# Cross-attention and a leaky-ReLU layer on one core: the state placed by matmuls, its load put behind x, and the copies of the first microseconds dealt out anew

## The chip, the core and the metric

The kernel runs on one core of a Trainium2 chip. The core has a matrix engine (TensorE; its rows in the profile are PE, and PEld for the loading of its weights), a vector engine (VectorE, DVE), a scalar engine (ScalarE, ACT), a general engine (GpSimd, POOL) and an engine that only issues transfers (SyncE, SP). Each works through its own list of instructions in order; semaphores order them against each other. TensorE writes to a small memory, PSUM, of eight banks for each of 128 partitions; VectorE and ScalarE copy its results on into the large memory, SBUF. Transfers (DMAs) between the chip's main memory and SBUF are issued by SP, ACT or POOL and carried out by 16 DMA engines. The metric is the time of one run in microseconds (us) on the device. A smaller time is better.

## The reference, cut to what matters

```python
B, H, S, Ns, D = (8, 8, 512, 32, 64)         # x: B,H,S,D   state: B,H,Ns,D
scores  = scale * x @ state^T                # softmax over the 32 state rows
xread   = softmax(scores)  @ state           # B,H,512,64
scores2 = scale * state @ x^T                # softmax over the 512 positions
sread   = softmax(scores2) @ x               # B,H,32,64
t = concat([xread, sread], axis=2), heads side by side   # (4352, 512)
h = t @ w_in                                 # w_in 512 x 2048
out = max(0.01 * h, h) @ w_out               # w_out 2048 x 512
```

All inputs and the output are fp32; the matmuls run on bf16 copies.

## The kernel before, in words

**Algebra.** The rows of `xread` are never formed. For each batch the kernel first makes M = state @ w_in, head by head, (`a_m`, in four column chunks of 512, each evicted by `m_evict`), and then h = softmax(scores) @ M (FF1). FF1 of one batch is 16 steps of 128 hidden columns; each result goes through a leaky ReLU on ScalarE into `hT`. The second matmul (FF2) is cut into pieces: `piece(b, hT, i, jq)` does four matmuls, a quarter jq of the sum for 128 output rows i, and with jq = 3 copies the finished 128 x 512 tile out and stores it. The `sread` rows of all batches are gathered and go through both layers at the end.

**Order.** The order is written by hand: inside `tc.manual_schedule` each engine runs its instructions as the program lists them. Batch 0 has its own opening (lines 403 to 554) and batch 1 its own passage (lines 556 to 597), because there is nothing yet to hide their softmax behind. Then comes FF1 of batch 1, in a loop of 16 steps that prepares batch 2 (lines 604 to 633), and from batch 2 on a regular loop. This change touches what runs up to the end of that first loop, near 63 us. The rest is the same in both kernels.

**Buffers.** A tile pool hands out buffers by tag. Tiles of one tag take turns in the pool's `bufs` buffers, and a tile that gives no tag goes by its name. The pool `consts` has `bufs=1`. So the two halves of batch 0's x, `xf[0]` and `xf[1]` (heads 0 to 3 and 4 to 7, 512 KB each, lines 62 to 68), have a buffer each, by the tags `xf0` and `xf1`. The whole state in fp32, `stf`, has the tag `xf1` too (line 110), and its load, which SP issues, comes after the casts that read `xf[1]`. PSUM is dealt out in the same way: tags `py` and `ph` with two banks of one tile each, `big` and `sc` with one tile of two banks each.

**Opening of batch 0.** ACT loads the state of batch 0 (`st0f`); SP loads `xf[0]` and `xf[1]`; POOL then issues the weights by a queue of its own, in this order: `w_in` chunks 0 and 1, 2 and 3, `w_out` chunk 0, x of batch 1, `w_out` 1, and later `w_out` 2 and 3 and x of batch 2. `spin` issues matmuls on zeros. `state0` transposes batch 0's state and places it in two forms: `st0_t`, heads stacked, and `stbd`, two heads as a block diagonal with zeros between (cleared by a memset). For each half u of x: `cast_x0` makes bf16, `x0_half` transposes it on TensorE, `xt0_evict` copies the transpose to SBUF, `scores0` multiplies it with `stbd`, and `max0`, `sub0`, `exp0`, `probs0` do the softmax. `at0_t` transposes the probabilities for FF1; the second half's feed the matmuls with g = 1 (`ff1_0(ph, 0, (1,))`, line 534). `a_scores(a0)` and `a_max2(a0)` begin the softmax over positions.

**State of all batches.** POOL casts `stf` twice into `stb` (line 538); within FF1 of batch 0 `state_t` transposes it in 16 matmuls, and VectorE copies it into `st_t` in two halves (line 154). Batch 1's M needs `st_t`.

**Batch 1.** M chunk 0, the cast of x, 16 transposes of x into one `big` tile, two copies to `xT`, the scores, the softmax (`a_shift`, `a_exp`, `a_probs`) and M chunks 1 to 3 stand between the FF2 pieces of batch 0. `a_probs(a1)` must be done before FF1 of batch 1.

Of the kernel before, what the change touches and what calls it, by code (L numbers as in the profile page):

```python
# [9 lines left out]
P = 128  # L10
B, H, S, D = 8, 8, 512, 64
NS = 32
# [3 lines left out]
NT = S // P  # L16
NK = H // 2
# [10 lines left out]
def kernel(  # L28
# [30 lines left out]
    nc.scalar.dma_start(  # L59
        st0f[:], state[0].rearrange("h n d -> (h n) d").rearrange("(p r) d -> p r d", r=2)  # L60
    )
    xf = [
        consts.tile([P, NK, 2 * P], FP32, name="xf", tag="xf0"),
        consts.tile([P, NK, 2 * P], FP32, name="xf", tag="xf1"),
    ]
    xv = x[0].rearrange("h (p t) d -> p h (t d)", t=NT)
    for u in range(2):
        nc.sync.dma_start(xf[u][:], xv[:, NK * u:NK * (u + 1)])

    idle = consts.tile([P, S], BF16, name="idle")  # L70
    nc.vector.memset(idle[:], 0.0)  # L71
    stbd = consts.tile([P, NK, 2, NS], BF16, name="stbd")
    nc.vector.memset(stbd[:], 0.0)
    warm = consts.tile([P, 2], FP32, name="warm")
    nc.vector.memset(warm[:], 0.0)
    nc.scalar.activation(out=warm[:], in_=warm[:], func=AF.Exp)
    ident = consts.tile([P, P], BF16, name="ident")
    make_identity(nc, ident[:])

    w_in_bf = wpool.tile([P, NK, DFF], BF16, name="w_in_bf")  # L80
    w_out_bf = wpool.tile([P, 16, DM], BF16, name="w_out_bf")
# [25 lines left out]
            moe_w_in[:, DM * c:DM * (c + 1)].rearrange("(k p) f -> p k f", p=P),  # L107
        )

    stf = consts.tile([P, 16, D], FP32, name="stf", tag="xf1")  # L110

    def load_state():
        nc.sync.dma_start(
            stf[:], state.rearrange("b h n d -> (b h n) d").rearrange("(p r) d -> p r d", r=16)
        )

    def load_w_out(c):
        nc.gpsimd.dma_start(
            w_out_bf[:, 4 * c:4 * (c + 1), :],
# [7 lines left out]

    st0_t = consts.tile([P, P], BF16, name="st0_t")  # L130
    st_t = consts.tile([P, B, P], BF16, name="st_t")
    sr_t = consts.tile([P, NK, B * NS], BF16, name="sr_t")

    def state0():
        stb0 = consts.tile([P, 2, 2, D], BF16, name="stb0")
        nc.gpsimd.tensor_copy(stb0[:], st0f[:, :, None, :].to_broadcast([P, 2, 2, D]))
        ps = psum.tile([P, 2, P], BF16, name="pst0", tag="big", bufs=1)
        for r in range(2):
            nc.tensor.transpose(ps[:, r, :], stb0[:, r].rearrange("p g d -> p (g d)"), ident[:])
        for g in range(2):  # L140
            rows = slice(D * g, D * (g + 1))
            src = ps[rows].rearrange("p r (k g q) -> p k g q r", k=NK, g=2)[:, :, g]
            VEC(stbd[rows, :, g].rearrange("p k (q r) -> p k q r", r=2), src)
            SCA(st0_t[rows, :].rearrange("p (k q r) -> p k q r", k=NK, r=2), src)

    stb = consts.tile([P, 16, 2, D], BF16, name="stb")

    def state_t():
        ps = psum.tile([P, 16, P], BF16, name="pst", tag="big", bufs=1)
        for r in range(16):  # L150
            nc.tensor.transpose(ps[:, r, :], stb[:, r].rearrange("p g d -> p (g d)"), ident[:])
        for g in range(2):
            rows = slice(D * g, D * (g + 1))
            nc.vector.tensor_copy(
                st_t[rows].rearrange("p b (k q r) -> p (b k) q r", k=NK, q=2),
                ps[rows].rearrange("p r (c g q) -> p c g q r", g=2, q=2)[:, :, g],
            )

# [25 lines left out]
        a_xt_pe(a, a.pxt, 0, NT)  # L186

    def st_of(a, g, k):
        rows, cols = slice(D * g, D * (g + 1)), slice(NS * k, NS * (k + 1))
        return st0_t[rows, cols] if a.b == 0 else st_t[rows, a.b, cols]  # L190

    def a_scores(a):
        sc = psum.tile([P, 2, S], FP32, name="sc", tag="sc", bufs=1)
# [208 lines left out]

    open_xb(0)
    a_open(a0, 0)
    spin(5, "py")
    state0()
    spin(4, "py")

    def x0_half(u):
        pxt = [psum.tile([P, NT, P], BF16, name="pxth", tag="ph") for _ in range(2)]  # L410
        for v in range(2):
            for t in range(NT):
                h = NK * u + 2 * v
                nc.tensor.transpose(
                    pxt[v][:, t, :], a0.xb[:, t, h:h + 2, :].rearrange("p h d -> p (h d)"), ident[:]
                )
        return pxt

    def xt0_evict(u, pxt):
        for v, copy in ((0, VEC), (1, SCA)):  # L420
            copy(a0.xT[:, :, 2 * u + v, :], pxt[v][:])

    sct = psum.tile([P, 2, NG, NS], FP32, name="sct", tag="sc", bufs=1)

    def scores0(u):
        for t in range(NT):
            for v in range(2):
                c = NK * t + 2 * v
                nc.tensor.matmul(
                    sct[:, u, c:c + 2, :].rearrange("p c n -> p (c n)"),  # L430
                    lhsT=a0.xT[:, t, 2 * u + v, :],
                    rhs=stbd[:, 2 * u + v].rearrange("p g n -> p (g n)"),
                    start=True, stop=True,
                )
# [36 lines left out]
    load_w_in(0)  # L471
    load_w_in(1)
    cast_x0(0, 2, VEC)
    cast_x0(2, 3, SCA)
    cast_x0(3, 4, POO)
    pxt = x0_half(0)
    xt0_evict(0, pxt)
    cast_x0(4, 6, VEC)
    cast_x0(6, 7, SCA)
    cast_x0(7, 8, POO)  # L480
    for c in range(2, 4):
        load_w_in(c)
    load_state()
    load_w_out(0)
    load_x(1, nc.gpsimd)
    load_w_out(1)
    scores0(0)
    pxt = x0_half(1)
    m = max0(0)
    xt0_evict(1, pxt)  # L490
    sub0(0, m)
    scores0(1)
    exp0(0)
    sub0(1, max0(1))
    spin(2, "ph")

    m_evict(a0, 0, a_m(a0, 0, "py"), SCA)
    exp0(1)
    spin(6, "ph")
    a_scores(a0)  # L500
    probs0(0)
    a0.aT = att.tile([P, 2, S], BF16, name="aT", tag="aT")
    pat = psum.tile([P, 2, 2 * S], BF16, name="pat", tag="big", bufs=1)
    at0_t(0, 0, NT, pat[:, 0])
    SCA(a0.aT[:, 0], pat[:, 0, :S])
    probs0(1)
    pm = a_m(a0, 1, "py")
    spin(2, "ph")

# [14 lines left out]

    ph = [psum.tile([P, S], FP32, name="ph", tag="ph")[:] for _ in range(2)]
    ff1_0(ph, 0, (0,))
    at0_t(1, 0, 2, pat[:, 0, S:])
    at0_t(1, 2, NT, pat[:, 1])  # L530
    VEC(a0.aT[:, 1, :2 * P], pat[:, 0, S:S + 2 * P])
    SCA(a0.aT[:, 1, 2 * P:], pat[:, 1, :2 * P])
    m_evict(a0, 1, pm, VEC)
    ff1_0(ph, 0, (1,))
    act_0(ph, 0)
    a_max2(a0)
    for g in range(2):
        POO(stb[:, :, g], stf[:])
    for c in range(2, 4):
        load_w_out(c)  # L540
    for j in range(2, 16, 2):
        if j % 4 == 2 and j < 12:
            pr = psum.tile([P, 2, S], FP32, name="php", tag="big", bufs=1)
            ff1_0([pr[:, 0], pr[:, 1]], j)
            nc.scalar.activation(out=h0[:, j:j + 2, :], in_=pr[:], func=AF.Prelu, alpha=0.01)
        else:
            ph = [psum.tile([P, S], FP32, name="ph", tag="ph")[:] for _ in range(2)]
            ff1_0(ph, j)
            act_0(ph, j)
        if j in (2, 6):  # L550
            c = 2 + j // 4
            m_evict(a0, c, a_m(a0, c, "py"), VEC)
        if j == 12:
            state_t()

    tags = ("py", "py", "ph", "ph")
    open_xb(1)
    a_open(a1, 1)
    for i in (0, 1):
        piece(0, h0, i, 0, tags[i])  # L560
    m_evict(a1, 0, a_m(a1, 0, "big"), SCA)
    for g in range(2):
        a_exp2(a0, g)
    cast_x(1, 0, 3, POO)
    cast_x(1, 3, 6, VEC)
    cast_x(1, 6, 8, SCA)
    load_x(2, nc.gpsimd)
    for i in (2, 3):
        piece(0, h0, i, 0, tags[i])
    a_xt_full(a1)  # L570
    VEC(a1.xT[:, 0:2], a1.pxt[:, 0:2])
    SCA(a1.xT[:, 2:4], a1.pxt[:, 2:4])
    piece(0, h0, 0, 1, tags[0])
    a_scores(a1)
    m_evict(a1, 1, a_m(a1, 1, "big"), SCA)
    a_shift(a1)
    a_max2(a1)
    for i in (1, 2):
        piece(0, h0, i, 1, tags[i])
    m_evict(a1, 2, a_m(a1, 2, "big"), SCA)  # L580
    a_exp(a1)
    a_probs(a1)
    for i, jq in ((3, 1), (0, 2)):
        piece(0, h0, i, jq, tags[i])
    m_evict(a1, 3, a_m(a1, 3, "big"), SCA)
    for g in range(2):
        a_exp2(a1, g)
    a_probs2(a0)
    a_a2t(a0)
    for i, jq in ((1, 2), (2, 2), (3, 2), (2, 3), (3, 3)):  # L590
        piece(0, h0, i, jq, tags[i], VEC if i % 2 else SCA)
    a_probs2(a1)
    a_a2t(a1)
    open_xb(2)
    cast_x(2, 0, 5, POO)
    cast_x(2, 5, 8, VEC)
    a_open(a2, 2)


# [5 lines left out]
    for s in range(16):  # L605
# [4 lines left out]
        if s == 2:  # L610
            a_xt_full(a2)
            VEC(a2.xT[:], a2.pxt[:])
        elif s == 4:
            a_scores(a2)
            m_evict(a2, 0, a_m(a2, 0, "big"), SCA)
            a_shift(a2)
            a_max2(a2)
            cast_x(3, 0, 8, POO)
        elif s == 7:
            m_evict(a2, 1, a_m(a2, 1, "big"), SCA)  # L620
        elif s == 8:
            a_exp(a2)
        elif s == 9:
            a_sread(a0)
        elif s in (10, 11):
            a_exp2(a2, s - 10)
            if s == 11:
                a_probs(a2)
                a_probs2(a2)
        elif s == 12:  # L630
            m_evict(a2, 2, a_m(a2, 2, "big"), SCA)
            a_open(att_of[3], 3)
            a_xt_dma(att_of[3])

# [99 lines left out]
```

## Time and profile before

| | us |
|---|---|
| median of three runs | 227.44 |
| the runs | 226.44, 227.44, 227.64 |
| the profiled execution | 227.53 |
| its span, first to last instruction | 225.8 |
| TensorE busy | 211.6 (94%) |
| ScalarE busy | 140.4 (62%) |
| VectorE busy | 102.9 (46%) |
| GpSimd busy | 23.9 (11%) |

A line of the timeline gives the start in us, the duration in us (of a group: from its first start to its last end), the engine, the line of the kernel, the operation, what is written and read, how many of them, and in brackets how long the engine stood idle before it and who released it. SPq, POOLq and ACTq are the issuing of transfers; their own duration is the issue, not the transfer. A line of waits gives the engine and line that waited, who ended the wait, the total in us, how often, and the longest.

### The profile page before, as it was taken

What the parts mean: (1) busy time and instruction counts of PE and PEld (TensorE: products, weight loads), DVE (VectorE), ACT (ScalarE), POOL (GpSimd) and SP (SyncE); (2) the same over time, 40 slices, a digit from 0 to 9 for tenths busy, and PEclk for the clock granted to TensorE, in tenths of its full rate; (3) what the DMA queues carried; (4) which work ended last, traced back from release to release, by engine and by line L of the source; (5) the groups of instructions that cost most, each with busy time, mean ns of one, the idle gap of its engine ahead of it and who ended that gap; (6) DMA issues with size and microseconds to landing.
All of it is one profiled execution on the core that took longest, in us unless ns stands there. A gap on an engine that the chain in (4) does not pass through costs nothing.

```text
span 225.8 us, 3512 instructions
## 1 busy us (share of the span) xinstructions
PE 211.6 (94%) x1411; PEld 98.4 (44%) x1437; DVE 102.9 (46%) x151; ACT 140.4 (62%) x262; POOL 23.9 (11%) x28
## 2 busy tenths in 40 slices
PE   7689978899899999999999999999999999999994
PEld 2333433344344444444444444444443444456653
DVE  2688428977846732673268327832782100000000
ACT  3448765658976846684668566865686465554420
POOL 5842202000221003000300030000000000000000
PEclk9889999999999999999999999999999999999999
DMA  6999990098591198119811892191213021102113
GB/s 195 186 250 273 221 281 6 1 194 274 103 270 46 49 202 216 49 46 184 235 49 46 168 218 83 46 163 26 93 51 93 0 93 49 46 1 92 49 46 93
DMA packets 35311, 27.02 MB, mean 120 GB/s; under 512 B 19808, under 2 KB 30432, under 8 KB 35296
## 3 DMA queue, kind: packets, MB, share of 16 engines
q1 hardware_dynamic: 30384, 20.45, 34.6%
q0 software_dynamic: 4768, 6.29, 13.9%
q8 instruction: 11, 0.18, 0.3%
q10 hardware_dynamic: 144, 0.07, 0.1%
q14 instruction: 4, 0.03, 0.1%
HBM read 17.37 MB, written 8.91 MB: 116 GB/s over the span
## 4 chain that ended last, share of the span: by engine, by line
PE 82%; ACT 7%; DVE 6%; DMA 2%; issue 2%; SPq 1%; POOL 0%; ACTq 0%; DVEq 0%
PE py L365 45%; PE ph L337 20%; PE pm L316 4%; PE ph L348 3%; PE pspin L126 2%; PE ph L518 2%; PE psr L290 1%; ACT M L330 1%; ACT hT L342 1%; PE sc L196 1%; DMA st0f<-in_state_dram 1%; ACT e L264 1%; PE pxt L178 1%; PE php L518 1%; DMA out_dram<-ysb 1%
## 5 line engine op out<-in xcount | busy, mean ns | idle before, releaser
L365 PE MATMUL py<-w_out_bf,hT 128*128 128x512 bf16 x478 | 122.9, 379 | 2.0 <-issue 1.3
L342 ACT ACTIVATE hT<-ph 128x512 bf16<-128x512 f32 x112 | 67.2, 602 | 45.4 <-PE ph L337 45.4
L365 PEld LDWEIGHTS <-hT 128*128 128x128 bf16 x496 | 46.3, 98 | 57.3 <-issue 6.6
L337 PE MATMUL ph<-aT,M 128*128 128x512 bf16 x218 | 65.0, 379 | 2.1 <-ACT hT L342 1.0
L337 PEld LDWEIGHTS <-M 128*128 128x128 bf16 x224 | 21.5, 98 | 28.8 <-issue 3.6
L371 ACT COPY ysb<-py 128x512 f32<-128x512 f32 x31 | 18.2, 586 | 11.6 <-PE py L365 11.6
L92 POOL CAST xb<-xl 128x2048 bf16<-128x2048 f32 (+2 forms) x7 | 11.6, 1653 | 104.7 <-DMA xl<-in_x_dram 75.2
L330 DVE CAST M<-pm 128x1024 bf16<-128x1024 f32 x10 | 12.3, 1225 | 21.9 <-PE pm L316 21.9
L393 DVE COPY ysh<-pyh 128x256 f32<-128x256 f32 x1 | 0.4, 424 | 44.8 <-PE pyh L388 44.8
L330 ACT CAST M<-pm 128x1024 bf16<-128x1024 f32 x18 | 18.2, 1013 | 3.8 <-PE pm L316 3.8
L206 DVE TRANSPOSE_TENSOR_REDUCE mrow<-sc 128x32 f32<-128x1024 f32 x7 | 8.8, 1250 | 23.2 <-PE sc L196 23.1
L228 DVE TRANSPOSE_TENSOR_REDUCE r<-e 128x32 f32<-128x1024 bf16 x7 | 8.7, 1244 | 10.7 <-ACT e L223 10.7
L316 PE MATMUL pm<-w_in_bf,st_t 64*32 64x512 bf16 x256 | 13.3, 389 | 0.0
L264 ACT ACTIVATE e<-sc,mcols 128x512 bf16<-128x512 f32 x16 | 11.1, 698 | 0.0
L256 DVE TENSOR_REDUCE mcol<-sc 128x2 f32<-128x1024 f32 x8 | 9.7, 1214 | 0.0
L126 PE MATMUL pspin<-idle 128*128 128x512 bf16 x18 | 7.7, 569 | 1.5 <-DVE idle L71 1.2
L352 ACT ACTIVATE hs<-ph 128x256 bf16<-128x256 f32 x16 | 6.0, 385 | 4.6 <-PE ph L348 4.4
L237 DVE STREAM_TRANSPOSE qb<-qh 128x1024 bf16<-128x1024 bf16 x7 | 8.7, 1246 | 0.2
L214 DVE STREAM_TRANSPOSE mrowb<-mrow 128x1024 f32<-128x1024 f32 x7 | 8.7, 1245 | 0.2
L216 DVE TENSOR_TENSOR sh<-sc,mrowb 128x1024 f32<-128x1024 f32 x7 | 8.6, 1224 | 0.2
L348 PE MATMUL ph<-sr_t,w_in_bf 128*128 128x256 bf16 x64 | 8.3, 273 | 0.0
L223 ACT ACTIVATE e<-sh 128x1024 bf16<-128x1024 f32 x7 | 7.4, 1051 | 0.4 <-DVE sh L216 0.4
(80 smaller groups left out, 144.3 us busy)
## 6 DMA issues: line engine op xcount, KB each, us to landing
out_dram<-ysb SPq DMA_DIRECT2D x31, 256.0 KB, 2.3
xl<-in_x_dram SPq DMA_DIRECT2D x5, 1024.0 KB, 7.0
w_in_bf<-in_moe_w_in_dram POOLq DMA_DIRECT2D x4, 512.0 KB, 8.2
w_out_bf<-in_moe_w_out_dram POOLq DMA_DIRECT2D x4, 512.0 KB, 14.1
xl<-in_x_dram POOLq DMA_DIRECT2D x2, 1024.0 KB, 12.6
xf<-in_x_dram SPq DMA_DIRECT2D x2, 512.0 KB, 4.6
stf<-in_state_dram SPq DMA_DIRECT2D x1, 512.0 KB, 6.4
out_dram<-ysb SPq DMA_DIRECT2D x8, 64.0 KB, 1.7
```

The costliest lines, as they stand in the source:

```text
L92: copy(xs[b][:, :, h0:h1].rearrange("p t h d -> p h t d"), xl[b][:, h0:h1].rearrange("p h (t d) -> p h t d", t=NT),)
L126: nc.tensor.matmul(p[:], lhsT=idle[:, :P], rhs=idle[:], start=True, stop=True)
L206: nc.vector.tensor_reduce(out=m1[:], in_=flat.rearrange("p (c j) -> p c j", j=NS), axis=AX.X, op=ALU.max, apply_transpose=True,)
L256: nc.vector.tensor_reduce(out=m2[:], in_=a.sc[:], axis=AX.X, op=ALU.max, negate=True)
L264: nc.scalar.activation(out=a.e2[:, g], in_=a.sc[:, g, :], func=AF.Exp, bias=a.m2s[:, g:g + 1], scale=SCALE, accum_out=a.r2[:, g:g + 1],)
L316: nc.tensor.matmul(at[v][NS * r:NS * (r + 1)], lhsT=st_of(a, g, k), rhs=w_in_bf[D * g:D * (g + 1), k, DM * c:DM * (c + 1)], start=True, st ...
L330: copy(a.M[:, :, cols], pm[:])
L337: nc.tensor.matmul(ph[:], lhsT=a.M[:, g, P * j:P * (j + 1)], rhs=a.aT[:, g, :], start=(g == 0), stop=(g == 1),)
L342: nc.scalar.activation(out=hT[:, j, :], in_=ph[:], func=AF.Prelu, alpha=0.01)
L348: nc.tensor.matmul(ph[:, :n], lhsT=w_in_bf[:, k, P * j:P * (j + 1)], rhs=sr_t[:, k, :], start=(k == 0), stop=(k == NK - 1),)
L365: nc.tensor.matmul(y.py[:], lhsT=hT[:, j, P * i:P * (i + 1)], rhs=w_out_bf[:, j, :], start=(j == 0), stop=(j == 15),)
L371: copy(ysb[:], y.py[:])
```

## The change

- `xf[0]` and `xf[1]` are given no tag; `stf` is given a tile of its own, and SP issues its load directly behind the two of x.
- `state0`: POOL casts `st0f` once; `identg` holds, for each g, the identity with the columns of the other heads set to zero (made on POOL); four matmuls against it replace two transposes, and one copy by ScalarE replaces two by VectorE and two by ScalarE. `st0_t` and the memset of `stbd` go; `st_of` reads `stbd` for batch 0.
- `state_t`: 32 matmuls with columns of the identity replace 16 transposes, into the tag `sc`; they stand ahead of batch 0's first `at0_t`. ScalarE makes `stb` in one cast in place of POOL's two, and `state_evict` is one VectorE copy within FF1 of batch 0.
- Batch 0's x: ScalarE casts heads 2 and 3; VectorE casts heads 4 to 6, POOL head 7. The halves' transposes use different PSUM tags; `scores0` runs through the first pair of heads before the second. Spins are moved.
- `a_scores(a0)` and `a_max2(a0)` move into FF1 of batch 0 (j = 8), as do chunks 0 and 1 of batch 1's M (j = 10 and 12), evicted by VectorE.
- Batch 1's x is transposed in two halves, in `big` and `sc`; `a_probs2(a0)` and the transpose by DMA behind it move to the end of the pieces, and `a_probs(a1)` ahead of six of them.
- `w_out` 1 to 3 and x of batch 2 are issued by POOL directly behind x of batch 1. POOL alone casts x of batch 2.
- In FF1 of batch 1, batch 2's M chunks 1 and 2 move from steps 7 and 12 (ScalarE) to 12 and 14 (VectorE).

```diff
-    xf = [
-        consts.tile([P, NK, 2 * P], FP32, name="xf", tag="xf0"),
-        consts.tile([P, NK, 2 * P], FP32, name="xf", tag="xf1"),
-    ]
+    xf = [consts.tile([P, NK, 2 * P], FP32, name="xf") for _ in range(2)]
     xv = x[0].rearrange("h (p t) d -> p h (t d)", t=NT)
     for u in range(2):
         nc.sync.dma_start(xf[u][:], xv[:, NK * u:NK * (u + 1)])
+    stf = consts.tile([P, 16, D], FP32, name="stf")
+    nc.sync.dma_start(
+        stf[:], state.rearrange("b h n d -> (b h n) d").rearrange("(p r) d -> p r d", r=16)
+    )
...
+    identg = consts.tile([P, 2, P], BF16, name="identg")
+    nc.gpsimd.memset(identg[:], 0.0)
+    for g in range(2):
+        nc.gpsimd.tensor_copy(
+            identg[:, g].rearrange("p (k v q) -> p k v q", k=NK, v=2)[:, :, g],
+            ident[:].rearrange("p (k v q) -> p k v q", k=NK, v=2)[:, :, g],
+        )
...
-    stf = consts.tile([P, 16, D], FP32, name="stf", tag="xf1")
...
     def state0():
-        stb0 = consts.tile([P, 2, 2, D], BF16, name="stb0")
-        nc.gpsimd.tensor_copy(stb0[:], st0f[:, :, None, :].to_broadcast([P, 2, 2, D]))
-        ps = psum.tile([P, 2, P], BF16, name="pst0", tag="big", bufs=1)
+        ps = psum.tile([P, 2, P], FP32, name="pst0", tag="big", bufs=1)
         for r in range(2):
-            nc.tensor.transpose(ps[:, r, :], stb0[:, r].rearrange("p g d -> p (g d)"), ident[:])
-        for g in range(2):
...
+            for g in range(2):
+                nc.tensor.matmul(
+                    ps[D * g:D * (g + 1), r, :], lhsT=stb0[:, r, :], rhs=identg[:, g, :],
+                    start=True, stop=True,
+                )
+        SCA(
+            stbd[:].rearrange("p k g (q r) -> p (k g) q r", r=2),
+            ps[:].rearrange("p r (h q) -> p h q r", q=16),
+        )
...
     def state_t():
-        ps = psum.tile([P, 16, P], BF16, name="pst", tag="big", bufs=1)
+        ps = psum.tile([P, 16, D], FP32, name="pst", tag="sc", bufs=1)
         for r in range(16):
-            nc.tensor.transpose(ps[:, r, :], stb[:, r].rearrange("p g d -> p (g d)"), ident[:])
...
+            for g in range(2):
+                nc.tensor.matmul(
+                    ps[D * g:D * (g + 1), r, :].rearrange("p (c q) -> p c q", q=2),
+                    lhsT=stb[:, r, :],
+                    rhs=ident[:].rearrange("p (c v q) -> p c v q", v=2, q=2)[:, :, g],
+                    start=True, stop=True,
+                )
+        return ps
+
+    def state_evict(ps, copy):
+        copy(
+            st_t[:].rearrange("p b (k q r) -> p (b k) q r", k=NK, q=2),
+            ps[:].rearrange("p r (c q) -> p c q r", q=2),
+        )
...
-    spin(5, "py")
+    POO(stb0[:], st0f[:])
+    spin(6, "py")
     state0()
-    spin(4, "py")
+    spin(3, "py")
...
     cast_x0(0, 2, VEC)
-    cast_x0(2, 3, SCA)
-    cast_x0(3, 4, POO)
+    cast_x0(2, 4, SCA)
     pxt = x0_half(0)
-    xt0_evict(0, pxt)
-    cast_x0(4, 6, VEC)
-    cast_x0(6, 7, SCA)
+    xt0_evict(0, pxt, (VEC, SCA))
+    cast_x0(4, 7, VEC)
     cast_x0(7, 8, POO)
     for c in range(2, 4):
         load_w_in(c)
-    load_state()
     load_w_out(0)
     load_x(1, nc.gpsimd)
-    load_w_out(1)
+    for c in range(1, 4):
+        load_w_out(c)
+    load_x(2, nc.gpsimd)
     scores0(0)
     pxt = x0_half(1)
     m = max0(0)
-    xt0_evict(1, pxt)
+    xt0_evict(1, pxt, (SCA, VEC))
     sub0(0, m)
+    spin(2, "ph")
     scores0(1)
     exp0(0)
+    SCA(stb[:], stf[:])
     sub0(1, max0(1))
-    spin(2, "ph")
+    exp0(1)
+    spin(5, "ph")
 
     m_evict(a0, 0, a_m(a0, 0, "py"), SCA)
-    exp0(1)
-    spin(6, "ph")
-    a_scores(a0)
+    pst = state_t()
     probs0(0)
...
-    spin(2, "ph")
...
     ff1_0(ph, 0, (0,))
-    at0_t(1, 0, 2, pat[:, 0, S:])
-    at0_t(1, 2, NT, pat[:, 1])
-    VEC(a0.aT[:, 1, :2 * P], pat[:, 0, S:S + 2 * P])
-    SCA(a0.aT[:, 1, 2 * P:], pat[:, 1, :2 * P])
+    at0_t(1, 0, NT, pat[0][:, 1])
+    VEC(a0.aT[:, 1], pat[0][:, 1, :S])
     m_evict(a0, 1, pm, VEC)
     ff1_0(ph, 0, (1,))
     act_0(ph, 0)
-    a_max2(a0)
-    for g in range(2):
-        POO(stb[:, :, g], stf[:])
-    for c in range(2, 4):
-        load_w_out(c)
+    open_xb(1)
+    a_open(a1, 1)
...
-        if j == 12:
-            state_t()
+            if j == 2:
+                state_evict(pst, VEC)
+        elif j == 8:
+            a_scores(a0)
+            a_max2(a0)
+        elif j in (10, 12):
+            c = (j - 10) // 2
+            m_evict(a1, c, a_m(a1, c, ("py", "big")[c]), VEC)
...
-    for i in (2, 3):
+    for i in (0, 1, 2):
         piece(0, h0, i, 0, tags[i])
-    a_xt_full(a1)
-    VEC(a1.xT[:, 0:2], a1.pxt[:, 0:2])
-    SCA(a1.xT[:, 2:4], a1.pxt[:, 2:4])
-    piece(0, h0, 0, 1, tags[0])
+    for t0, tag, copy in ((0, "big", VEC), (2, "sc", SCA)):
+        ps = psum.tile([P, 2, NK, P], BF16, name="pxt2", tag=tag, bufs=1)
+        a_xt_pe(a1, ps, t0, t0 + 2)
+        copy(a1.xT[:, t0:t0 + 2], ps[:])
+    piece(0, h0, 3, 0, tags[3])
     a_scores(a1)
...
     a_exp(a1)
-    a_probs(a1)
...
     for g in range(2):
         a_exp2(a1, g)
+    a_probs(a1)
+    for i, jq in ((0, 2), (1, 2), (2, 2), (3, 2), (2, 3), (3, 3)):
+        piece(0, h0, i, jq, tags[i], VEC if i % 2 else SCA)
     a_probs2(a0)
     a_a2t(a0)
...
-    cast_x(2, 0, 5, POO)
-    cast_x(2, 5, 8, VEC)
+    cast_x(2, 0, 8, POO)
...
-        elif s == 7:
-            m_evict(a2, 1, a_m(a2, 1, "big"), SCA)
...
-        elif s == 12:
-            m_evict(a2, 2, a_m(a2, 2, "big"), SCA)
-            a_open(att_of[3], 3)
-            a_xt_dma(att_of[3])
+        elif s in (12, 14):
+            c = s // 2 - 5
+            m_evict(a2, c, a_m(a2, c, "big"), VEC)
+            if s == 12:
+                a_open(att_of[3], 3)
+                a_xt_dma(att_of[3])
```

## The prediction

> **What bounds the kernel now.** I read the page's busy shares and slices first, then the timeline of the first 63 us, the landings of each load, and TensorE's waits from 17 to 64 us.
>
> ```profile
> PE   7689978899899999999999999999999999999994
> DVE  2688428977846732673268327832782100000000
> PEclk9889999999999999999999999999999999999999
> ```
>
> From about 63 us TensorE is full, and nothing the change touches runs there. All it can move is the stretch before: an opening, up to 17.21 us, in which a chain of small copies sets the pace, and a passage in which TensorE works with a few waits. The opening in the timeline:
>
> ```profile
> 0.74 1.01 SPq L68 DMA_DIRECT2D xf<-in_x_dram  x2
> 5.34 0.43 DVE L99 CAST xb<-xf 128x512 bf16<-128x512 f32 x1
> 6.38 0.40 POOL L99 CAST xb<-xf 128x256 bf16<-128x256 f32 x1 [0.37 <-DMA xf<-in_x_dram]
> 7.35 0.41 ACT L99 CAST xb<-xf 128x256 bf16<-128x256 f32 x1
> 7.83 0.34 SPq L113 DMA_DIRECT2D stf<-in_state_dram  x1
> 7.92 0.69 DVE L443 TENSOR_REDUCE m<-sct 128x16 f32<-128x512 f32 x1 [0.63 <-PE sct L429]
> 8.86 0.68 DVE L448 TENSOR_TENSOR sh<-sct,m 128x512 f32<-128x512 f32 x1
> 14.30 2.48 POOL L538 CAST stb<-stf 128x1024 bf16<-128x1024 f32 x2 [3.56 <-DMA stf<-in_state_dram]
> 14.39 1.49 DVE L462 TENSOR_TENSOR at<-e,q 128x512 bf16<-128x512 bf16 x1
> 17.21 0.59 PE L518 MATMUL ph<-aT,M 128*128 128x512 bf16 x2 [0.86 <-ACT aT L532]
> 28.12 0.95 DVE L92 CAST xb<-xl 128x768 bf16<-128x768 f32 x1
> ```
>
> The second half of x lands at 6.38 (POOL waits for it). VectorE then runs almost unbroken from 7.92 to 15.88: maxima, subtractions, sums, products, the last one 1.49 beside POOL's casts where its twin took 0.69. FF1's second half starts at 17.21. See also that SP issues `stf` at 7.83, 0.07 after ScalarE's cast of `xf[1]` ends (7.76): it waited for that buffer. From issue to landing, the two x loads, and `stf`:
>
> ```profile
> DMA to landing us min/median/max: 4.2/4.6/5.1
> ```
> ```profile
> DMA to landing us min/median/max: 6.4/6.4/6.4
> ```
>
> TensorE's waits behind the opening are batch 1's:
>
> ```profile
> PE ph L337 <- ACT hT L342: 1.0, 2, 0.7
> PE pxt L178 <- ACT xb L92: 1.0, 1, 1.0
> PE sc L196 <- ACT xT L572: 1.0, 1, 1.0
> PE ph L337 <- DVE ysb L371: 0.9, 1, 0.9
> ```
>
> **The change, part by part.** All times against the profiled 227.53 (span 225.8, 1.73 around it; the median of the runs is 0.09 lower).
>
> *1. One buffer for x: +5.1.* Without tags both `xf` tiles go by one name in a pool with one buffer. SP can't issue `xf[1]` until both casts of `xf[0]` are done, and `stf` queues behind it. `xf[0]` lands at 0.74 + 4.2 = 4.94. ScalarE by then has placed the state: `st0f` landed at 3.46, one smaller POOL cast (under 0.40), four matmuls of 0.107 in place of two, one copy of 256 columns near 0.40 (its cast of that size took 0.41): about 4.9. Its cast of 512 columns takes 0.62 (its row in batch 1): 5.62. SP wakes 0.07 later: 5.69. For the transfer I take `stf`'s 6.4, the nearest row: same size, same queue, also issued into `w_in` loads in flight; so 12.1. The low end is the first x load's 4.2 (9.9). The high end lets `xf[1]` begin only when `w_in` 1 is through: that lands at 4.66 + 7.3 = 11.96 before, plus 1.43 for 512 KB (the x halves landed at 4.94 and 6.37): 13.4. VectorE's cast of three heads costs 0.95 (the 128x768 row), not 0.43: 13.05. VectorE's list holds `max0(0)` behind this cast, so the finished first half waits as well: `max0(0)` starts at 13.0 in place of 7.92. TensorE's list stands at the transposes of the second half, ScalarE's at their copy; `stf`, behind `xf[1]` on SP, lands 1.4 later, near 13.5, and ScalarE reaches its cast only near 15.8.
>
> The Trainium skill, DMA: Bandwidth & Descriptors, Queues, rings and completion order, says that each DMA engine takes turns between its queues by packet. By that rule `xf[1]` would start at once at half rate, 1.43 more than the first load's 4.2, landing near 11.3, and the sum would be 0.8 less. `stf`'s row speaks for the later landing.
>
> *POOL's queue* is held by the cast of head 7 up to 12.5, and with it `w_in` 2 and 3, `w_out` 0 to 3 and both x loads. Taking 5.5 for the first (`w_in` 0's row) and the spacing of before, `w_in` 2 lands near 18 (needed at 23), `w_out` 0 at 23 (31), x of batch 1 at 26 (31), x of batch 2 at 36.5 (48). All hidden, by 5 us or more.
>
> *2. The rest of the opening: -0.4.* From `max0(0)` to FF1's second half was 9.29. POOL's casts beside the product go: -0.80. One copy of `aT` in place of two in turn (0.29, 0.37): -0.38. TensorE stood idle for over 5 us, so the eight transposes take 0.86, not 0.61, their copy goes after `max0(0)`, and `sub0(0)` starts 1.47 after it, not 0.94: +0.53; slow scores +0.25. Hidden behind VectorE's 8 us: the spins, M chunk 0 (0.54 to 1.04), ScalarE's cast of `stb` (about 1.05, as its 128x1024 rows) and 32 matmuls of `state_t`. These lie between 16 x 0.056 and 32 x 0.056 us (0.9 to 1.8) at full clock; I take 1.3, ending 0.1 after the probabilities. FF1's second half then starts at 17.21 + 4.7 = 21.9.
>
> *What can hold that up is the clock,* here by the microsecond (the column behind the engines' busy times is the granted clock):
>
> ```profile
> 10.00:11.00 1.00, 1.00 (x6) 0.13 (x8) 0.94 (x2) 0.20 (x1) 0.74 (x1) 0.51 1.26 211
> ...
> 13.00:14.00 1.00, 1.00 (x12) 0.27 (x10) 0.97 (x3) 0.00 (x0) 0.00 (x0) 0.79 1.13 263
> 14.00:15.00 1.00, 1.00 (x20) 0.34 (x12) 0.93 (x3) 0.35 (x1) 0.70 (x1) 1.00 1.24 207
> ```
>
> It fell to half at 10.0 and rose at 13.4 (0.79 is the mean of that microsecond); in the first microseconds the transposes at 5.87 still took 0.107 each, 4.7 after the first spin. If full clock comes at 16.8, one more such step of 3.4, 3.7 after TensorE's work begins anew at 13.1, nothing is added; if 5.6 (first spin to last slow transpose, 1.19 to 6.8), TensorE's list is late by about 1.2. I take the first for the sum and the second for the range.
>
> The Trainium skill, TensorE: Matmul & The Clock Gate, part 1, speaks against the change: an idle window of some 3.4 us halves the clock, and it comes back only after a busy one, at a phase that differs by run. By it the delay lies between 0 and 1.6.
>
> *3. FF1 of batch 0: -0.4.* `state_t` and its wait go (1.05 + 0.2), `a_scores(a0)` (0.24) and two chunks of M (0.35 each) come; ScalarE's sixteen Preludes (8.6) bound the rest, now with smaller gaps.
>
> *4. The pieces: -1.75.* Two chunks of M gone, -0.7. The wait for ScalarE's cast falls from 1.0 to 0.25, that for `xT` from 1.1 to 0.4: -1.45. VectorE's softmax of batch 1 (3.8 + 3.85, with ScalarE's exp held by M chunk 3 between) becomes the last: FF1 of batch 1 waits 0.8 where it waited 0.4: +0.4.
>
> *5. -0.9:* the last `ysb` copy no longer queues behind both `a_probs2`.
>
> *6. FF1 of batch 1: +0.5.* ScalarE loses two evictions of 1.0, and with them the waits of 0.34 and 0.67: -1.0. But M chunk 1 of batch 2 now queues on VectorE behind `a_probs` and `a_probs2`, which ended at 61.2 in the timeline before; 1.28 for the eviction makes `big` free at 62.5, while TensorE was done with step 14 at 60.7, and chunk 2 behind it needs `big`. That is 1.8; the exp ahead of `a_probs` comes some 0.3 earlier without ScalarE's eviction: +1.5.
>
> `identg` (three small POOL writes before 3.5 us) lies under the wait for `st0f`, 2.2 long.
>
> Sum: 5.1 - 0.4 - 0.4 - 1.75 - 0.9 + 0.5 = +2.15, so 227.53 + 2.15 = 229.7.
>
> **The rivals.**
>
> *A. The halves overlap after all* (the untagged tiles are two buffers, or the wait is otherwise absent). For it: nothing in the profile shows an untagged pair. Against: `stf` at 7.83 shows how this pool makes a tile wait. x lands at 6.4, the cast of 0.95 ends at 7.85, part 1 is 0, FF1 starts about 0.2 after 17.21: 227.53 + 0.2 - 0.4 - 1.75 - 0.9 + 0.5 = 225.2. It decides if SP issues `xf[1]` before 3 us. This one is faster.
>
> *B. The delay is absorbed:* `xf[1]` lands at 9.9, and the clock is up early. Part 1 shrinks by 2.2, of which up to 0.5 goes to TensorE's slow list: about 228.0. For it: the low end of the transfer. Against: two `w_in` loads are ahead.
>
> *C. The clock comes late* (or `xf[1]` at 13.4): +1.2 to +1.3, about 230.9. For it: 5 us of idle TensorE is longer than the gaps that dropped the clock at 10 us.
>
> **How the numbers follow.** Main case 0.52, A 0.08, B 0.18, C 0.22. The predicted time is the main case's, 229.7. It alone could lie between 228.7 and 230.5 (0.9 for where batch 1's waits fall, and the 0.1 to 0.8 of the transfer). The range reaches through B to half way to A, and past C by the 0.9: 226.6 to 232.0. Half a per cent, 1.1 us, is about what a measurement tells from no change. Slower than 228.6: all of C, nearly all of the main case, little of B: 0.70. Faster than 226.3: A and a little: 0.12. The rest 0.18.
>
> **What would show it.** SP issues `xf[1]` near 5.7 with a wait ahead, and `stf` behind it; VectorE stands idle before a 128x768 cast near 12; TensorE has a gap of some 5 us before 13, and a second stretch of halved clock; FF1's second half at 21 to 23; the waits of 1.0 for `xb` and `xT` shrink; a wait of over 1 us on `big` in line `a_m` near 62 to 64. The prediction is wrong if the x loads stand together at 0.74, or if the passage from FF1 to step 0 of batch 2's FF1 (45.6 before) takes more than 45 or less than 40.

## The result and the profile after

The changed kernel takes 233.21 us (median of four runs: 232.26, 232.29, 234.14, 234.22) against 226.95 beside it: a ratio of 1.0274, 95% interval 1.0205 to 1.0343. It is slower. The forecast said slower, 229.7, within 226.6 to 232.0; the measured time lies above that range.

The page of the changed kernel opens with these slices (busy tenths, 40 slices of 5.8 us). TensorE's second and third digit are 1 and 4 where they were 6 and 8: the hole in the opening. The clock's second and third digit, 7 and 5, and its twelfth, 7, are two stretches at half speed; the kernel before had one, short, in the opening.

```profile
PE   7147999989969999999999999999999999999994
DVE  1048884879956652666266527652764200000000
PEclk9759999999979999999999999999999999999999
```

The opening in the timeline of the changed kernel (start, duration, engine and line, idle time before with what ended it). The first line groups both loads of x: 5.34 is the time from the first issue at 0.74 to the end of the second.

```profile
0.74 5.34 SPq L65 DMA_DIRECT2D xf<-in_x_dram  x2
6.13 0.63 SPq L67 DMA_DIRECT2D stf<-in_state_dram  x1
13.82 0.95 DVE L105 CAST xb<-xf 128x768 bf16<-128x768 f32 x1 [7.42 <-DMA xf<-in_x_dram]
14.69 0.68 DVE L453 TENSOR_REDUCE m<-sct 128x16 f32<-128x512 f32 x1
14.83 1.03 PE L424 MATMUL pxth<-ident,xb 128*128 128x128 bf16 x8 [7.70 <-DVE xb L105]
23.69 0.59 PE L527 MATMUL ph<-aT,M 128*128 128x512 bf16 x2 [0.59 <-DVE aT L539]
```

The answers for the two load lines give the issues and landings; of `xf[1]` it is the last issue and the longest landing, of `stf` the other line:

```profile
L65 SPq DMA_DIRECT2D xf<-in_x_dram x2: 384/422/459, 0.7 to 5.7; - x2
...
DMA to landing us min/median/max: 4.3/6.2/8.1
...
DMA to landing us min/median/max: 8.9/8.9/8.9
```

So SP issues the second half of x at 5.7, not at 1.3, and it lands 8.1 us later. The maxima of the first half, ready since 7.1, start at 14.69.

The wait in the opening and TensorE's waits behind it are these (total, times, longest), and the two rows below, from the timeline, belong to the second of them:

```profile
PE pxth L424 <- DVE xb L105: 7.7, 1, 7.7
PE pm L325 <- DVE M L339: 2.0, 1, 2.0
PE ph L346 <- DVE aT L247: 0.7, 1, 0.7
PE sc L205 <- ACT xT L577: 0.2, 1, 0.2
```
```profile
64.89 1.22 DVE L339 CAST M<-pm 128x1024 bf16<-128x1024 f32 x1
...
66.16 0.50 PE L325 MATMUL pm<-w_in_bf,st_t 64*32 64x512 bf16 x8 [2.00 <-DVE M L339]
```

The waits of 1.0 for `xb`, `xT` and `ysb` are gone; a new one of 2.0 stands at M chunk 2 of batch 2. What follows it is in the stretches of 1 us there (busy time of TensorE, its weight loads, VectorE, ScalarE, GpSimd; then the granted clock, DMA share, GB/s):

```profile
64.00:65.00 1.00, 0.15 (x1) 0.09 (x1) 0.93 (x6) 0.60 (x1) 0.00 (x0) 1.00 1.17 212
65.00:66.00 1.00, 0.00 (x0) 0.00 (x0) 1.00 (x1) 0.00 (x0) 0.00 (x0) 1.00 0.94 175
66.00:67.00 1.00, 0.84 (x10) 0.25 (x10) 0.40 (x2) 0.00 (x0) 0.00 (x0) 0.68 0.83 268
67.00:68.00 1.00, 1.00 (x4) 0.45 (x3) 0.93 (x1) 0.34 (x1) 0.00 (x0) 0.50 0.96 293
```

Stage by stage, profiled run against profiled run (starts of the named instructions; step 1 of batch 1's FF1 is the second one):

| stage | before | after | difference | predicted |
|---|---|---|---|---|
| 1. start to `max0(0)` | 7.92 | 14.69 | +6.8 | +5.1 |
| 2. to FF1's second half | 9.29 | 9.00 | -0.3 | -0.4 |
| 3. FF1 of batch 0, to the first piece | 9.07 | 9.56 | +0.5 | -0.4 |
| 4. the pieces, to FF1 of batch 1 | 17.41 | 15.48 | -1.9 | -1.75 |
| 5. its step 0 to step 1 | 1.52 | 0.59 | -0.9 | -0.9 |
| 6. step 1 to step 0 of batch 2's FF1 | 17.65 | 19.80 | +2.15 | +0.5 |
| to its step 1 | 1.30 | 1.62 | +0.3 | 0 |

Together +6.6, the difference of the spans (232.4 and 225.8). The profiled run is one of the two near 234.2; the other two have spans of 230.5.

### The profile page after: what moved, and what is told of

It is laid out like the page before. It is cut to its first block, busy times and chain, and to the rows that moved or that the text cites. A ratio compares the mean times of both kernels' runs of the same rounds, so it can differ in the third digit from the quotient of the medians.

```text
span 232.4 us, 3532 instructions
## 1 busy us (share of the span) xinstructions
PE 212.0 (91%) x1426; PEld 98.4 (42%) x1452; DVE 105.3 (45%) x151; ACT 137.0 (59%) x256; POOL 22.1 (10%) x28
## 4 chain that ended last, share of the span: by engine, by line
PE 80%; DVE 8%; DMA 6%; ACT 3%; issue 1%; SPq 0%; ACTq 0%; DVEq 0%
PE py L374 46%; PE ph L346 20%; DMA xf<-in_x_dram 5%; PE pm L325 4%; PE ph L357 3%; PE ph L527 2%; PE psr L299 1%; PE sc L205 1%; DVE qb L246 1%; DVE r L237 1%; PE php L527 1%; PE pxt L187 1%; ACT e L232 1%; DMA out_dram<-ysb 1%; DVE aT L247 1%
## 5 line engine op out<-in xcount | busy, mean ns | idle before, releaser
L374 PEld LDWEIGHTS <-hT 128*128 128x128 bf16 x496 | 46.8, 98 | 58.2 <-issue 7.7
L339 DVE CAST M<-pm 128x1024 bf16<-128x1024 f32 x13 | 15.9, 1224 | 22.5 <-PE pm L325 22.5
L98 POOL CAST xb<-xl 128x2048 bf16<-128x2048 f32 (+1 forms) x7 | 12.2, 1741 | 109.6 <-DMA xl<-in_x_dram 47.4
L339 ACT CAST M<-pm 128x1024 bf16<-128x1024 f32 x14 | 14.2, 1013 | 3.7 <-PE pm L325 3.6
L325 PE MATMUL pm<-w_in_bf,st_t 64*32 64x512 bf16 x224 | 10.5, 385 | 2.1 <-DVE M L339 2.0
L273 ACT ACTIVATE e<-sc,mcols 128x512 bf16<-128x512 f32 x16 | 11.1, 698 | 0.0
L424 PE MATMUL pxth<-ident,xb 128*128 128x128 bf16 x16 | 1.7, 266 | 7.7 <-DVE xb L105 7.7
L125 PE MATMUL pspin<-idle 128*128 128x512 bf16 x15 | 6.5, 561 | 1.4 <-DVE warm L74 1.2
```

Of the source, the lines that this page charges most:

```text
L98: copy(xs[b][:, :, h0:h1].rearrange("p t h d -> p h t d"), xl[b][:, h0:h1].rearrange("p h (t d) -> p h t d", t=NT),)
L273: nc.scalar.activation(out=a.e2[:, g], in_=a.sc[:, g, :], func=AF.Exp, bias=a.m2s[:, g:g + 1], scale=SCALE, accum_out=a.r2[:, g:g + 1],)
L325: nc.tensor.matmul(at[v][NS * r:NS * (r + 1)], lhsT=st_of(a, g, k), rhs=w_in_bf[D * g:D * (g + 1), k, DM * c:DM * (c + 1)], start=True, st ...
L339: copy(a.M[:, :, cols], pm[:])
L374: nc.tensor.matmul(y.py[:], lhsT=hT[:, j, P * i:P * (i + 1)], rhs=w_out_bf[:, j, :], start=(j == 0), stop=(j == 15),)
```

## The experiments

Two questions were open: whether the shared buffer is all of the loss, and what made stages 1 and 6 dearer than predicted.

**1. Two buffers in the changed kernel.**

```diff
-    xf = [consts.tile([P, NK, 2 * P], FP32, name="xf") for _ in range(2)]
+    xf = [consts.tile([P, NK, 2 * P], FP32, name="xf", tag=f"xf{u}") for u in range(2)]
```

> The changed kernel with a tag, and so a buffer, of its own for each half of x; nothing else. Theory one: nearly all of the loss is the second half of x waiting for the first half's buffer. Then the second half lands near 6.4 us instead of 13.8, VectorE's first maximum starts near 7.9 instead of 14.7, the 5 us gap of TensorE goes, and the time falls by 6 to 8 us to 225.5 (224.5 to 227), a little under the kernel before. Theory two: the new opening (state_t and the cast of stb ahead of the probabilities, three heads cast by VectorE) is what costs. Then the time stays above 230 us.

Measured: 224.68 us (224.48 to 224.73), ratio to the kernel before 0.9874 (0.9847 to 0.9902). In its timeline SP issues both halves at the start, the second cast comes at 6.90 and the maxima at 7.76:

```profile
0.74 1.01 SPq L65 DMA_DIRECT2D xf<-in_x_dram  x2
1.80 0.50 SPq L67 DMA_DIRECT2D stf<-in_state_dram  x1
6.90 0.94 DVE L105 CAST xb<-xf 128x768 bf16<-128x768 f32 x1
7.76 0.68 DVE L453 TENSOR_REDUCE m<-sct 128x16 f32<-128x512 f32 x1
16.30 0.59 PE L527 MATMUL ph<-aT,M 128*128 128x512 bf16 x2 [0.59 <-DVE aT L539]
```

With one argument the change turns from a loss of 2.7% into a gain of 1.3%. Taken together, the rest of it is worth having; the shared buffer alone costs the changed kernel 8.5 us.

**2. One buffer in the kernel before.** The two tags of `xf` are left out, nothing else. `stf` keeps the tag `xf1`, which no other tile uses now.

```diff
-    xf = [
-        consts.tile([P, NK, 2 * P], FP32, name="xf", tag="xf0"),
-        consts.tile([P, NK, 2 * P], FP32, name="xf", tag="xf1"),
-    ]
+    xf = [consts.tile([P, NK, 2 * P], FP32, name="xf") for _ in range(2)]
```

> The kernel before with the two tags of xf taken away, nothing else. Theory one: the load of the second half is issued near 5.7 to 6 us, lands near 13 to 14, and the time rises by 5 to 7.5 us to 232 to 234.5. Theory two: the time stays within 1 us of 227.

Measured: 234.70 (234.37 to 235.26), ratio 1.0319 (1.0285 to 1.0353). SP issues the second half at 6.37, it lands 7.7 later, and the wait is the same one; the maxima start at 14.42, FF1's second half at 24.94 (7.92 and 17.21 before):

```profile
PE pxth L411 <- DVE xb L96: 6.1, 1, 6.1
```

The buffer is enough to make the loss in either kernel.

**3. Two of batch 2's copies of M back on ScalarE.** The changed kernel, with M chunks 1 and 2 of batch 2 at steps 7 and 12 on ScalarE as before.

```diff
+        elif s == 7:
+            m_evict(a2, 1, a_m(a2, 1, "big"), SCA)
...
-        elif s in (12, 14):
-            c = s // 2 - 5
-            m_evict(a2, c, a_m(a2, c, "big"), VEC)
-            if s == 12:
-                a_open(att_of[3], 3)
-                a_xt_dma(att_of[3])
+        elif s == 12:
+            m_evict(a2, 2, a_m(a2, 2, "big"), SCA)
+            a_open(att_of[3], 3)
+            a_xt_dma(att_of[3])
```

> The changed kernel with batch 2's M chunks 1 and 2 evicted by ScalarE at steps 7 and 12 again, as before the change. Theory one: TensorE's wait of 2.0 us near 66 us comes from VectorE's queue, and the halved clock behind it (66.4 to 69.8 us) from the wait. Then both go, ScalarE's waits of 0.3 and 0.7 come back, and the time falls by 1.5 to 3 us to 230.2 to 231.7. Theory two: the wait only moves to another place in the same stretch; the time stays within 0.8 us of 233.2.

Measured: 231.77 (231.62 to 231.83), ratio 1.0187 (1.0159 to 1.0215). The wait of 2.0 is gone, and ScalarE's waits of the kernel before are back:

```profile
PE ph L346 <- ACT hT L351: 1.2, 2, 0.7
```

Step 1 of batch 1's FF1 to step 0 of batch 2's takes 17.64 (19.80 in the changed kernel, 17.65 before), and the clock stays full there. The four runs lie within 0.2 of each other, not in two pairs.

**4. Both mends together:** two buffers, and the copies as in 3.

> Both edits together: a buffer for each half of x, and batch 2's M chunks 1 and 2 on ScalarE. Theory one: the two losses are separate and add up, about 223.8 us (223 to 225), faster than the kernel before. Theory two: with the opening quick again VectorE has no backlog at step 14, and this equals the run with two buffers alone within 0.5 us.

Measured: 224.12 (224.05 to 224.40), ratio 0.9855 (0.9821 to 0.9889). With two buffers the copies' place is worth only 0.56, between the two theories, where it was worth 1.4 with one. In experiment 1 TensorE waits 1.6 at the same place, the clock does not fall, and the stage takes 18.11; here it takes 17.65.

**5 and 6. What made the transfer take 8.1 us.** The changed kernel, with `w_in` 1, and then `w_in` 0 too, issued behind POOL's cast of head 7:

```diff
-    load_w_in(0)
-    load_w_in(1)
+    load_w_in(0)        # in 6 not here either
...
     cast_x0(7, 8, POO)
-    for c in range(2, 4):
+    for c in range(1, 4):        # in 6: range(4)
         load_w_in(c)
```

> The changed kernel with the load of w_in 1 put behind POOL's cast of head 7, so that only w_in 0 is ahead of the second half of x. Theory (a newly issued load begins when the load in progress, w_in 0, has ended near 9.3 us, and then shares packet by packet with whatever is next): nothing is next here, so the 512 KB take 1.43 us alone, and the half lands near 11.2 in place of 13.8; max0(0) starts near 12.1 and the time falls by about 2.5 us, to 230.7. Rival (8 us is what this transfer costs whatever is ahead of it, because the queue takes that long to start or because its packets are slow): it still lands at 13.8, time 233.2. Second rival (it is shared with everything in flight from its issue on): with w_in 0 alone beside it, it would land at 5.65 + 4.2 + 1.43, about 11.3 as well, but its first packet is seen near 7, not at 9.3.

> The changed kernel with both w_in 0 and w_in 1 put behind POOL's cast of head 7: no load is ahead of the second half of x. Theory (it waits only for a load in progress): first packet about 2.5 us after the issue at 5.65, landing after 4.2 to 4.6 us, near 10.0, max0(0) near 10.9, 3.8 us earlier than in the changed kernel, time about 229.4. w_in 0, issued near 10.4, lands 5.5 later at 16, before its matmuls near 15.5 to 17: at most 0.5 of that is lost. Rival (the delay of 3.8 us before the first packet is the queue's own start): as with one load ahead, landing near 11.2, time near 230.7.

Measured: 229.87 (229.68 to 232.67) and 228.99 (228.41 to 229.50); ratios 1.0128 (1.0078 to 1.0179) and 1.0073 (1.0050 to 1.0095). The maxima start at 12.04 and at 10.23, for 14.69 in the changed kernel. One of the four runs of 5, that of 232.67, has a lower mean clock than the others (0.978 against 0.984 to 0.985); no trace of it was kept. The second half is issued at 5.7 to 5.8 in all three; VectorE's cast of it, in 5 and then in 6, starts as it lands:

```profile
11.17 0.95 DVE L105 CAST xb<-xf 128x768 bf16<-128x768 f32 x1 [4.32 <-DMA xf<-in_x_dram]
```
```profile
9.36 0.95 DVE L105 CAST xb<-xf 128x768 bf16<-128x768 f32 x1 [2.90 <-DMA xf<-in_x_dram]
```

The packets of the transfers, counted from the traces' records by the microsecond in which they start ("x" is SP's queue, where `xf[1]` has 512 packets of 1 KB; "weights" is POOL's, also 1 KB each; from 13 us on in the changed kernel, 10 in 5 and 8 in 6, SP's include the first of `stf`):

```
us from              5    6    7    8    9   10   11   12   13
changed  weights    25   98  204  204  170  121  119  102   13
         x           0    0    0    0   54  121  119  170  155
5        weights    10  104  202  198   14    0    0    2   50
         x           0    0    0   17  344  234   77    0    0
6        weights     0    0    0    0    0    0   21  161  199
         x           0   22  262  285   95    8    0    0    0
```

The 8.1 us come apart into three. **Until the first packet:** 1.05 after the issue with nothing ahead (6), 3.1 in 5, 3.8 in the changed kernel. **The transfer itself:** with the engines to itself it takes 2.1 and 1.8 (6 and 5). In the changed kernel it goes one for one with the packets of `w_in` 1 (121 and 121, 119 and 119 in a microsecond) and takes 3.9: one of its packets takes 46 ns alone, one of the weights takes 98. **To be seen by VectorE:** 0.4.

So the numbers that the theory gave were nearly met (landing near 11.1 for 11.2; 9.4, where 10.0 was expected), and a fixed price falls. The words of the theory, that a new load begins when the running one ends, hold in 5: the first packet at 8.82 comes with the first engine to finish `w_in` 0, and sharing from the issue on is out. Experiment 2 speaks against them: there `w_in` 0 is through on all engines at 9.3, and the second half's first packet comes at 10.26. What fits all is the time since the issue: 3.8 (changed; 3.7 in the traces of experiments 3 and 7, whose openings are the same), 3.9 (experiment 2) and 3.7 (`stf` in the kernel before, issued at 7.83, first packet at 11.49), all with the weights' queue never empty; 3.1 where it ran empty first. Why a new load is held off so long, and then shares evenly, no run here shows.

The times fell by 3.3 and 4.2. In 6 the maxima come 4.5 earlier, of which FF1's second half keeps 3.9: `w_in` 1 is late there, by 0.8 at M chunk 1.

**7. Does the clock fall because TensorE waits?** The changed kernel, with TensorE kept busy on zeros in the wait.

```diff
             c = s // 2 - 5
+            if s == 14:
+                spin(8, "ph")
             m_evict(a2, c, a_m(a2, c, "big"), VEC)
```

> The changed kernel with eight matmuls of zeros (8 x 0.216 = 1.73 us) on TensorE ahead of M chunk 2 of batch 2, where it waited 2.0 us for the buffer. Theory (the second stretch of halved clock at 66 us follows from that wait, and makes the difference between the runs at 232.3 and those at 234.2): TensorE waits only some 0.3 us there, the clock stays full, and all runs lie near 232.3, that is 0.9 below the median of the changed kernel, with no pair 1.9 us apart. Rival (the clock drops there for a reason other than the wait, and the wait itself of 2.0 is the whole loss): the drop is still seen in some runs, the times still lie in two groups, and the median stays at 233.2.

Measured: 232.35, five runs between 232.16 and 232.55. Nothing useful was added, and the upper pair is gone, as the theory said. With experiment 3 that makes nine runs without it where the gap is filled or gone; two of the changed kernel's four have it. In its timeline the zeros fill the wait:

```profile
63.96 0.59 PE L346 MATMUL ph<-aT,M 128*128 128x512 bf16 x2
64.39 1.89 PE L125 MATMUL pspin<-idle 128*128 128x512 bf16 x8
66.21 0.41 PE L325 MATMUL pm<-w_in_bf,st_t 64*32 64x512 bf16 x8
```

M chunk 2 starts when it did (66.21 against 66.16), takes 0.41 and not 0.50, and step 0 of batch 2's FF1 comes at 67.85 in place of 69.12. From M chunk 2 on the changed kernel's profiled run is 1.3 slower here and 0.3 more a step later: 1.6 for the clock. The stage takes 18.13, +0.48 against the kernel before, where +0.5 was predicted.

The remaining 0.35 of the stage is not the clock. In the changed kernel a small operation of VectorE, ahead of both copies in its list, took 0.79, and here 0.35:

```profile
60.86 0.79 DVE L241 TENSOR_SCALAR r<-r 128x32 f32<-128x32 f32 x1
61.25 0.35 DVE L241 TENSOR_SCALAR r<-r 128x32 f32<-128x32 f32 x1
```

In both it ends 0.03 to 0.04 after POOL's cast of the x of batch 3 (59.72 to 61.61, and 59.67 to 61.57), and so it does in experiments 1, 5, 6 and 9; where that cast is over before it starts, as in experiment 3 (61.35, then 61.69), it takes 0.18. So TensorE's gap itself differs from run to run: 2.00 in the changed kernel and 2.05 in experiment 9, both with the clock falling behind it, and 1.8, 1.6 and 1.6 in experiments 5, 6 and 1, with no fall. The two groups of the changed kernel, 1.9 apart, are what the clock's 1.6 and this 0.35 make together, but no run of the lower group was traced, so whether its gap was shorter stays open.

**8. The copies on VectorE, at another place in its list.** Two buffers, chunk 1 at step 7 and chunk 2 at step 12, both on VectorE.

```diff
+        elif s == 7:
+            m_evict(a2, 1, a_m(a2, 1, "big"), VEC)
...
+        elif s == 12:
+            m_evict(a2, 2, a_m(a2, 2, "big"), VEC)
```

> The changed kernel with two buffers for x, and batch 2's M chunk 1 at step 7 and chunk 2 at step 12, both copied by VectorE: chunk 1 in the 1.07 us in which VectorE waits for ScalarE's exp, chunk 2 in the 4 us behind its softmax. Theory (the loss in FF1 of batch 1 is a matter of which engine's list the copy stands in, not of its cost): neither the wait for big (1.6 to 2.0) nor ScalarE's 1.2 us of waits remains; step 0 of batch 2's FF1 comes 0.5 to 1.0 earlier than with the copies on ScalarE, time 223.3. Rival (chunk 1 on VectorE holds up the softmax behind it, and so aT of batch 2): the wait for aT or for M grows by what is gained, time 224.1 or more.

Measured: 223.86 (223.79 to 225.14), ratio 0.9853 (0.9822 to 0.9884). The rows of VectorE show chunk 1 just ahead of the softmax's sum, and TensorE has one new wait:

```profile
51.83 1.22 DVE L339 CAST M<-pm 128x1024 bf16<-128x1024 f32 x1
52.96 1.24 DVE L237 TRANSPOSE_TENSOR_REDUCE r<-e 128x32 f32<-128x1024 bf16 x1
```
```profile
PE psr L299 <- DVE M L339: 0.8, 1, 0.8
```

Neither wait of the theory is left, but `a_sread(a0)` at step 9 now waits 0.8 for the same buffer, so the stage takes 17.31, only 0.3 less than with ScalarE. Two of the six runs lie at 225.12 and 225.14 with a mean clock of 0.992, the other four at 223.79 to 223.87 with 0.997 or more; where the clock fell in the two, no trace shows. Both versions beat both kernels. They differ by 0.26 in runs made at different times, which does not tell one from the other.

**9. Batch 1's M all in the pieces again.** Two buffers, and M chunks 0 and 1 of batch 1 taken out of batch 0's FF1.

```diff
-        elif j in (10, 12):
-            c = (j - 10) // 2
-            m_evict(a1, c, a_m(a1, c, ("py", "big")[c]), VEC)
...
-    for i in (0, 1, 2):
+    for i in (0, 1):
         piece(0, h0, i, 0, tags[i])
+    m_evict(a1, 0, a_m(a1, 0, "big"), SCA)
+    piece(0, h0, 2, 0, tags[2])
...
     a_scores(a1)
-    m_evict(a1, 2, a_m(a1, 2, "big"), SCA)
+    m_evict(a1, 1, a_m(a1, 1, "big"), SCA)
...
```

Chunks 2 and 3 each move on by three pieces.

> The changed kernel with two buffers for x, and batch 1's M chunks 0 and 1 taken out of batch 0's FF1 and put back among the pieces, copied by ScalarE as in the kernel before; everything else of the pieces as changed. With two buffers and M begun in FF1 the stretch from FF1's second half to the first piece took 9.56 us and the pieces to batch 1's FF1 15.47, time 224.68. Theory (beginning M in FF1 only moves 0.7 to 0.9 us from the pieces to a stretch that is itself full; what shortens the pieces is the casts and copies): FF1 takes 8.7 here and the pieces 16.2 to 16.4, the time stays within 0.5 of 224.7. Rival (M in FF1 is what makes room on ScalarE and VectorE for the casts and copies): FF1 takes 8.7, but the pieces go back to 17 or more, with waits on ScalarE in front of the transposes and scores, and the time is 225.4 or more.

Measured: 227.39 (225.57 to 228.35, ten runs), ratio 0.9975 (0.9940 to 1.0010). FF1 takes 9.38 here (17.00 to 26.38) and 9.56 with the two chunks in it, so they cost it 0.18, not the 0.9 that both theories gave. The row of TensorE says why: it waits for ScalarE's Preludes there in any case.

```profile
25.25 1.30 PE L527 MATMUL ph<-aT,M 128*128 128x512 bf16 x4 [0.74 <-ACT hT L534]
```

The pieces take 16.13, 0.66 more, with a wait of 0.7 for a copy of M ahead of the transposes, and step 0 of batch 1's FF1 takes 0.94 for 0.60. That is 0.8 net. The theory that the move is worth nothing falls; that it makes room for the casts holds in part. The median says more than it should: in the profiled run the clock fell behind a wait of 2.05 at M chunk 2 of batch 2, as in the changed kernel, and it rose late in the opening, which put FF1's second half at 17.00 (16.30 in experiment 1). The four runs with a mean clock of 0.997 or more lie between 225.57 and 226.46, 0.9 to 1.8 above experiment 1; the other six, at 0.990 to 0.992, between 227.16 and 228.35.

## Why the prediction fell short

**Direction and mechanism held.** The untagged pair is one buffer, SP waits for the casts of `xf[0]`, and the finished first half waits in VectorE's list behind the second half's cast. SP's issue at 5.70 was predicted as 5.69. Rival A's price for two buffers, 225.2, was measured as 224.68, in part by luck: FF1's second half came at 16.30, where its sum has 17.4, and FF1 itself took 0.5 more than before, not 0.4 less. Rival B, that the delay is absorbed, is out: nothing of it was.

**Step 1, "One buffer for x: +5.1", was mis-sized: +6.8.** The failing term is "For the transfer I take `stf`'s 6.4, the nearest row: same size, same queue, also issued into `w_in` loads in flight". It was 8.1, past even the high end (13.4, against a cast at 13.82). Both waited as long for their first packet, 3.7 and 3.8. What the row does not share is the packet: `stf` comes in 128 packets of 4 KB, `xf[1]` in 512 of 1 KB. Between its first packet and its last 172 packets of the weights start beside `stf` in the kernel before, and 408 beside `xf[1]`. `stf` takes 2.4 us there, where it takes 1.7 to 1.8 with the engines to itself (experiments 5 and 6); `xf[1]` takes 3.9, against 1.8 to 2.1. That the size of the packets makes this difference is read from these counts; no run changes it alone.

The rule weighed there (the Trainium skill, DMA: Bandwidth & Descriptors, Queues, rings and completion order: turns between queues by packet) agrees with the trace from 9.5 us on, 121 packets against 121. The working made "half rate" of it, and 30 packets in a quarter of a microsecond, where there are 95 alone, are a third. From 5.7 to 9.5 no turns are seen at all, and the landing at 11.3 that came of the rule was 2.5 early.

**Step 2 held (-0.3 for -0.4).** Full clock came at 18.6 in the changed kernel, later than the 16.8 taken. In experiments 1, 4 and 8, at full clock from 6.3 to 6.5 on, the stage takes 8.4 to 8.5 where it takes 9.0 here; so the late clock, or what else comes late with the load, cost some 0.5, and the rest of the stage gained more than was forecast. That the sum came out is in part luck. The 32 matmuls of `state_t` took 0.70, less than the 0.9 that was the low end.

**Step 3, "FF1 of batch 0: -0.4", was +0.5.** It credited `state_t` with 1.25. In the kernel before those matmuls stood where TensorE waits for ScalarE anyway. ScalarE, which bounds the stage, stood idle 0.81 behind them, and still 0.68 without them, in the changed kernel (second row) and in experiment 9 alike:

```profile
26.26 1.08 ACT L525 ACTIVATE hT<-ph 128x512 bf16<-128x512 f32 x2 [0.81 <-PE ph L518]
33.23 1.09 ACT L534 ACTIVATE hT<-ph 128x512 bf16<-128x512 f32 x2 [0.68 <-PE ph L527]
```

So their going freed 0.13, not 1.25. New are 0.44 of ScalarE's idle time behind `a_scores(a0)`, and 0.18 for the two chunks of M: +0.49 in all. Where one engine bounds a stage, work taken from another is worth only what it held up.

**Steps 4 and 5 held** (-1.9 for -1.75, -0.9 for -0.9). Of step 4, the two chunks of M were put at 0.7; experiment 9 shows 0.66.

**Step 6, "+0.5", held in its own terms and missed the clock.** The wait was 2.0, where 1.8 was predicted, and the net loss at full clock 0.48 (experiment 7; 0.46 in experiment 1). The prediction looked for the clock's behaviour in the opening alone, where TensorE was to stand idle, and not at the new gap it had itself put at 62 to 64. There the clock fell in the profiled run, which cost 1.6 us, and by the mean clocks and times in one more of the four (0.971 and 0.968, against 0.983 and 0.978). The Trainium skill, TensorE: Matmul & The Clock Gate, part 1, names a whole idle window of some 3.4 us; here a gap of 2.0 was enough: of the 3.4 us before the drop at 66.35 TensorE worked in 1.4. Gaps of 1.6 to 1.8 (experiments 1, 5 and 6) did not do it in the traced runs.

The missing 4.4 us of the profiled run are thus 1.7 of the transfer, 0.9 of FF1 and 2.0 in step 6 and the step behind it (1.6 for the clock, 0.35 for VectorE's small operation), less 0.1 elsewhere. The prediction's own sign of being wrong was met: from FF1's second half to step 0 of batch 2's FF1 took 45.4, more than the 45 that it named and far from the 43.1 that its terms make. Rival C added 1.2 for a clock that comes late in the opening; the sum came nearer to it for other reasons.

## What to carry to other kernels

A tile without a tag shares its name's buffers: read every list of tiles made in a loop for how many buffers it has, and find the load in the issuing engine's list that would wait. The price of a transfer behind others is not that of its bytes: count the time to its first packet from a row with the other queue as busy, and then its packets, one of the other queue's for each. Every wait of TensorE near 2 us should be priced twice, as the wait and as the clock that may fall behind it; filling it with matmuls on zeros went with a median 0.9 us lower.

## What was not expected

A load issued while the other queue was full of packets had its first packet 3.7 to 3.9 us later, in five profiles of three kinds of opening, for 1.05 with the other queue empty. It stood in the kernel before, unseen, inside the 6.4 of `stf`.

A gap of 2.0 us in TensorE, far from the opening, was followed by 3.4 us at half the clock. The same kernel's times stand in two groups 1.9 us apart (232.3 and 234.2), of which the upper shows the lower mean clock. A median of four such runs is a matter of how many fall on each side.

The length of that gap hung on a VectorE operation that takes 0.18 us by itself and up to 0.84 (experiment 9) when it starts beside a cast on POOL: in seven traces it ended 0.03 to 0.04 after the cast did.

The 32 matmuls of `state_t` with 64 columns each took 0.70 in all, 0.022 each; the shorter bound of the prediction was 0.9.
